# Holding back the fetches of the turned rows until the second and the fourth product of the second layer are computed

## The chip, the cores and the metric

One core of a Trainium2 chip runs the whole kernel. The metric is device time in microseconds (us), the median of several executions of the same program. TensorE (PE), VectorE (DVE), ScalarE (ACT) and GpSimd (POOL) each work through their own list of instructions in order; SyncE (SP) issues nearly all transfers (DMA), also in order. Between the engines stand semaphores. A matmul takes its stationary operand in a weight load (PEld) and streams the other one; all matrices are float32.

## The reference

Attention with random features, then a Fourier mix with a two-layer network, on 8 batches of 576 rows and 512 columns:

```
q_p, k_p = phi(q * scale), phi(k * scale)      # exp(h - max h), h = x @ omega.T - |x|^2 / 2
x   = (q_p @ (k_p.T @ v)) / (q_p @ sum(k_p) + 1e-6)      # heads side by side: (8, 576, 512)
u   = x + real(fft(fft(x, axis=1), axis=2))
un  = (u - mean(u)) / sqrt(var(u) + 1e-6)      # by rows
out = u + max(un @ w_ch1, 0) @ w_ch2           # w_ch1: 512 x 2048, w_ch2: 2048 x 512
```

## The kernel before

**Two stages.** The first stage (to about 424 us) does attention, the Fourier mix, the conversion of the weights and the network for the first 512 rows. The second stage does the network for the other 4096 rows, in eight blocks `j` of 512 rows. The change touches the second stage alone.

**A block.** Each layer of the network is one step of Strassen's scheme in Winograd's form: seven products of half-size matrices in place of eight, with sums of operands before and after. The first layer of a block (`first_of`, matmuls at L1310) goes through eight column groups `fc`, seven small products each. The second layer (`product_of`, matmuls at L1490) has seven products `i`, in the order `ORDER = (1, 2, 4, 5, 6, 7, 3)`, and each of these is once more split into seven **parts** `n`, in the order `PARTS = (1, 2, 5, 6, 3, 7, 4)`. "Part 4.1" is part n = 1 of product i = 4. So a block has 49 parts; a part is four matmuls (eight instructions in the trace, two passes of float32) and takes 0.893 us. Parts of neighbouring products are interleaved, and the first parts of a block's second layer run among the last products of its first layer; the next block's first layer starts among the last parts.

**Weights of the second layer.** The 49 pieces of a block's weights (256 KB each) are laid out in DRAM (`w2l`) and loaded anew for each block by `loads_w2` (issues at L1393, tile `wl`), product by product; loads are numbered #0 to #48 here, so #14 is part 4.1, #15 is 4.2, #28 is 6.1, #29 is 6.2 and #35 is 7.1. There are 12 buffers: load #n waits on SP until the (n-11)th part of the block in the order of execution has read its buffer.

**Operands of the parts.** Parts 5, 6, 7 and 3 of a product use four sums s1, s2, s3 and again s1, made by DVE in `add_up` (L1457). The last of them overwrites s1 and so must wait until part 5 has read it:

```
(s1, a(1, 0), a(1, 1), ALU.add, 5),
(s2, s1, a(0, 0), ALU.subtract, 6),
(s3, a(0, 0), a(1, 0), ALU.subtract, 7),
(s1, a(0, 1), s2, ALU.subtract, 3),
...
after = ready(0, 1) + ((me, "p5 read"),) * (n == 3)
```

So part 3 of a product needs: end of part 5, then one DVE addition of 128x512, then its own start. The results of the parts leave PSUM by ACT (L1465, L1523) and by DVE additions `added` (L1470). Whole products are added up by `plus` (L1530): 128x512 additions on POOL or DVE, POOL's starting as soon as ACT has written the last quarter of the product (L1523) and DVE the others.

**The turned rows.** The first layer needs the normalised rows transposed. For blocks 1 to 7 `norm_of` loads 128 rows (L1015), normalises them, DVE transposes 32x32 squares and SP stores the result in a DRAM tensor `turned` (L980). Once two such stores are done, `fetched(j, h, dst)` brings one half of the block back, reordered: four transfers of 128 KB (issues at L988, tile `unT`) for h = 0 and four for h = 1. Then `block_norms` makes four sums of the halves on DVE (L1171, tile `tt`), which the first layer of block j uses. The halves and the sums live in four slabs that come free when the first layer of block j - 1 ends; so both fetches, and the sums, take place during the second layer of block j - 1.

**What sets the order.** The kernel writes the whole order itself. Each piece of work is a `Step` with an engine, a planned duration, a planned delay of its result (`late`), the events it comes `after`, and for DMAs a size. `Listing.run` picks the step that could begin first by its own clock and appends it to its engine's list. `port=True` marks additions that the plan never lets DVE and POOL do at the same moment. The plan's events and times order the instructions; they do not become waits on the chip. There, semaphores are set only where data or buffers require it.

In the order before, the fetches of block j stand in SP's list directly behind load #13 (h = 0) and load #14 (h = 1) of the second layer of block j - 1.

Of the kernel before, what the change touches and what calls it, by code (L numbers as in the profile page):

```python
# [35 lines left out]
PE, ACT, DVE, POOL, SP, NONE = "pe", "act", "dve", "pool", "sp", "none"  # L36
# [244 lines left out]
def kernel(  # L281
# [685 lines left out]
    turned = {}  # L967
# [13 lines left out]

    def fetched(j, h, dst):
        yield Step(
            SP, 1.7, 3.0, after=(("turned", j, 2 * h), ("turned", j, 2 * h + 1)),
            makes=("unT", j, h), kb=330,
        )
        for g in range(4):
            nc.sync.dma_start(  # L988
                dst[Q * g : Q * g + Q].rearrange("q (b k) d t -> q b (k d t)", k=2),
                turned[j, h][:, g].rearrange("(b q) k n -> q b (k n)", q=Q),  # L990
            )
# [159 lines left out]
    def block_norms(j, pool):  # L1151
        t0 = (NPLAIN * TP + TB * j) // 128
        yield Step(NONE, take=("slab",) * 4, after=events_of(range(t0, t0 + TB // 128)) + ("converted",))
        un = unTs[j] = [slabs.tile([128, HT // Q, NDC, Q], F32, name="unT2", tag="slab") for _ in range(2)]
        tt = [slabs.tile([128, 2, HT // Q, D2, Q], F32, name="tt", tag="slab") for _ in range(2)]
        tts[j] = tt[0][:, 0], tt[0][:, 1], tt[1][:, 0]
        for i in range(TB // 128):
            h, k = divmod(i, HT // 128)
            if pool is mlpp:
                dst = un[h][:, 4 * k : 4 * k + 4].rearrange("p g d q -> p d g q")  # L1160
                yield Fork(norm_of(j, t0 + i, i, pool, dst))
            elif not k:
                yield Fork(fetched(j, h, un[h]))
        parts = TB // 128 if pool is mlpp else 2
        yield Step(NONE, after=tuple(("unT", j, i) for i in range(parts)), bias=1.54)
        ops = sums_right(
            un[0][:, :, 0:D2], un[1][:, :, 0:D2], un[0][:, :, D2:NDC], un[1][:, :, D2:NDC], *tts[j]
        )
        for i, (o, l, r, op) in enumerate(ops):
            yield Step(DVE, 0.6, makes=("tt", j) if i == 3 else None, port=True, bias=-0.49)  # L1170
            nc.vector.tensor_tensor(out=o, in0=l, in1=r, op=op)  # L1171
# [460 lines left out]
```

## Time and profile before

| | |
|---|---|
| median of 3 runs | 1171.0 us (1168.07 to 1171.58) |
| the profiled execution | 1174.67 us, span 1172.2 us |
| TensorE busy | 1153.5 us, 98% of the span; granted clock 0.996 |
| DVE, ACT, POOL busy | 64%, 37%, 37% |
| second stage, first to last matmul | 423.9 to 1167.8 us |
| part matmuls (L1490) | 3136 instructions, 275 ns mean, one every 0.112 us |
| DMA moved | 220.34 MB, mean 188 GB/s |

The busy share of a matmul engine whose instructions overlap says little on what it lost. In this kernel the losses of TensorE are read from the length of equal stretches of work: the same 368 instructions of the second layer take 41.1 us in one block and more in others.

### The profile page before, as it was taken

What the parts mean: (1) busy time and instruction counts of PE and PEld (TensorE: products, weight loads), DVE (VectorE), ACT (ScalarE), POOL (GpSimd) and SP (SyncE); (2) the same over time, 40 slices, a digit from 0 to 9 for tenths busy, and PEclk for the clock granted to TensorE, in tenths of its full rate; (3) what the DMA queues carried; (4) which work ended last, traced back from release to release, by engine and by line L of the source; (5) the groups of instructions that cost most, each with busy time, mean ns of one, the idle gap of its engine ahead of it and who ended that gap; (6) DMA issues with size and microseconds to landing.
All of it is one profiled execution on the core that took longest, in us unless ns stands there. A gap on an engine that the chain in (4) does not pass through costs nothing.

```text
span 1172.2 us, 31328 instructions
## 1 busy us (share of the span) xinstructions
PE 1153.5 (98%) x12437; PEld 1032.9 (88%) x12437; DVE 754.7 (64%) x1573; ACT 436.8 (37%) x1485; POOL 430.4 (37%) x496
## 2 busy tenths in 40 slices
PE   8999999999999999999999999999999999999998
PEld 7888888779777868998998998898999899899898
DVE  5999999986676655744754664573573574474255
ACT  6998898866444212122112212212212212221211
POOL 2433444455472106225225324413513512522421
PEclk8999999999999999999999999999999999999999
DMA  7866765665662254873783593694495396388055
GB/s 218 224 188 186 240 181 178 203 210 163 207 196 101 77 162 139 263 264 85 222 278 112 172 308 99 152 317 141 112 319 190 82 290 231 83 258 263 35 166 203
DMA packets 167217, 220.34 MB, mean 188 GB/s; under 512 B 50080, under 2 KB 81056, under 8 KB 167072
## 3 DMA queue, kind: packets, MB, share of 16 engines
q1 hardware_dynamic: 166576, 218.09, 60.7%
q8 instruction: 98, 1.61, 0.6%
q14 instruction: 47, 0.39, 0.1%
q10 hardware_dynamic: 496, 0.26, 0.1%
HBM read 179.24 MB, written 43.25 MB: 190 GB/s over the span
## 4 chain that ended last, share of the span: by engine, by line
PE 88%; DMA 5%; DVE 4%; ACT 2%; SPq 1%; issue 1%; DVEq 0%
PE banks L1310 33%; PE banks L1490 27%; PE banks L1099 5%; PE banks L606 5%; PE banks L1122 4%; PE banks L512 4%; DMA wl<-w2l 3%; PE banks L640 2%; PE banks L687 2%; PE banks L849 2%; PE banks L799 1%; ACT e L566 1%; DVE nmx L549 1%; DMA kq<-in_k_dram 1%; PE banks L809 1%; PE banks L860 1%
## 5 line engine op out<-in xcount | busy, mean ns | idle before, releaser
L1490 PE MATMUL banks<-wl,sums 128*128 128x128 f32 x1792 | 217.4, 275 | 0.0
L1490 PEld LDWEIGHTS banks<-wl,sums 128*128 128x128 f32 x1792 | 208.6, 192 | 0.0
L1296 DVE CUSTOM_DVE_ANT_0 hid<-banks,s 128x256 f32<-128x256 f32 x192 | 80.9, 424 | 188.8 <-PE banks L1310 188.8
L566 ACT ACTIVATE e<-banks,nmx 128x128 f32<-128x128 f32 x576 | 165.3, 434 | 23.2 <-DVE nmx L549 22.4
L1324 ACT ACTIVATE s<-banks 128x256 f32<-128x256 f32 x192 | 73.7, 384 | 259.0 <-PE banks L1310 259.0
L1310 PE MATMUL banks<-unT,w 128*128 128x256 f32 x704 | 166.3, 379 | 0.0
L1310 PEld LDWEIGHTS banks<-unT,w 128*128 128x128 f32 x704 | 133.2, 190 | 18.3 <-issue 0.5
L1530 POOL TENSOR_TENSOR ur<-ur,part 128x512 f32<-128x512 f32 x32 | 47.3, 1479 | 267.1 <-ACT part L1523 187.0
L1465 ACT ACTIVATE s<-banks 128x128 f32<-128x128 f32 x168 | 46.6, 278 | 256.7 <-PE banks L1490 220.3
L1310 PE MATMUL banks<-tt,w1s 128*128 128x256 f32 x512 | 126.3, 379 | 0.0
L1310 PEld LDWEIGHTS banks<-tt,w1s 128*128 128x128 f32 x512 | 97.0, 190 | 13.7 <-DVE hid L1296 0.4
L1490 PE MATMUL banks<-wl,hid 128*128 128x128 f32 x768 | 100.0, 276 | 3.2 <-DMA wl<-w2l 3.1
L1470 DVE TENSOR_TENSOR part<-banks,s 128x128 f32<-128x128 f32 x168 | 49.0, 292 | 83.4 <-PE banks L1490 82.2
L549 DVE TENSOR_REDUCE nmx<-banks 128x8 f32<-128x1024 f32 (+1 forms) x96 | 89.3, 951 | 19.7 <-PE banks L606 15.5
L1490 PEld LDWEIGHTS banks<-wl,hid 128*128 128x128 f32 x768 | 94.0, 192 | 6.0 <-DMA wl<-w2l 4.5
L606 PE MATMUL banks<-om,kqT 64*64 64x128 f32 (+1 forms) x2088 | 80.6, 278 | 1.9 <-ACT kv L656 1.2
L1310 PE MATMUL banks<-unT,w1s 128*128 128x256 f32 x320 | 79.5, 379 | 0.0
L606 PEld LDWEIGHTS banks<-om,kqT 64*64 64x64 f32 (+1 forms) x2088 | 65.8, 140 | 13.3 <-issue 4.3
L1490 PE MATMUL banks<-wl,hs 128*128 128x128 f32 x576 | 75.1, 275 | 0.5 <-DVE part L1470 0.4
L1490 PEld LDWEIGHTS banks<-wl,hs 128*128 128x128 f32 x576 | 70.1, 192 | 1.2 <-DVE part L1470 0.6
L1377 POOL TENSOR_TENSOR hs<-hid,hs 128x256 f32<-128x256 f32 x64 | 50.1, 784 | 57.2 <-issue 37.1
L1310 PEld LDWEIGHTS banks<-unT,w1s 128*128 128x128 f32 x320 | 60.4, 190 | 8.7
(128 smaller groups left out, 1914.6 us busy)
## 6 DMA issues: line engine op xcount, KB each, us to landing
wl<-w2l SPq DMA_DIRECT2D x392, 256.0 KB
raw<-in_moe_w_ch_dram SPq DMA_DIRECT2D x32, 512.0 KB
kq<-in_k_dram SPq DMA_DIRECT2D x32, 288.0 KB
kq<-in_q_dram SPq DMA_DIRECT2D x32, 288.0 KB
vd<-in_v_dram SPq DMA_DIRECT2D x32, 288.0 KB
u<-us SPq DMA_DIRECT2D x36, 256.0 KB
ur<-us SPq DMA_DIRECT2D x36, 256.0 KB
out_dram<-ur SPq DMA_DIRECT2D x34, 256.0 KB
```

Source lines behind the costliest of these rows:

```text
L512: nc.tensor.transpose(ps[:, (j - j0) * 128 : (j - j0 + 1) * 128], src(j), ident[:])
L549: nc.vector.tensor_reduce(nmx[:, :, 0:num], pps[:, :, 0 : MF * num].rearrange("p b (c m) -> p b c m", m=MF), axis=AX.X, op=ALU.max, negate ...
L566: nc.scalar.activation(out=e[:, c + (i if num == 1 else 0), :], in_=pps[:, i, MF * c : MF * c + MF], func=AF.Exp, bias=nmx[:, i, c : c + 1],)
L606: nc.tensor.matmul(pps[cols, c, MF * m : MF * m + MF], lhsT=kqT[rows, j, cols], rhs=om2[rows, :],)
L1099: nc.tensor.matmul(hp[:, 0:TP], lhsT=w1[:, dc, 128 * fc : 128 * fc + 128], rhs=unTs[key][:, dc, :], start=(dc == 0), stop=(dc == NDC - 1),)
L1296: nc.vector._custom_dve(TENSOR_ADD_SAT, out=o, in0=ps, in1=sb, s0=FMAX, s1=0.0)
L1310: nc.tensor.matmul(ps[:, 0:HT].rearrange("f (b q) -> f b q", q=Q), lhsT=left(dc), rhs=right(dc), start=start and dc == 0, stop=(dc == D2 - 1),
L1324: nc.scalar.activation(out=s[:], in_=ps[:, 0:HT], func=AF.Copy)
L1377: nc.gpsimd.tensor_tensor(out=o, in0=l, in1=r, op=op)
L1470: nc.vector.tensor_tensor(out=part[:, t, 128 * m : 128 * m + 128], in0=ps[:, 0:128], in1=saved[with_][:], op=ALU.add,)
L1490: nc.tensor.matmul(ps[:, 0:128], lhsT=left[:, f], rhs=wls[j, i, n][:, f], start=start and f == 0, stop=(f == 3), skip_group_check=True,)
L1530: eng.tensor_tensor(out=o, in0=o, in1=other, op=ALU.add)
```

## The change

The planned step of a fetch gets one more event to come after: the reading of product 2 of the running second layer for h = 0, of product 4 for h = 1 (`"read"` is made by the last part of a product; by `ORDER` these are the second and the third product to be computed). Its planned time on SP goes from 1.7 to 1.9 and its planned delay from 3.0 to 5.0.

```diff
     def fetched(j, h, dst):
         yield Step(
-            SP, 1.7, 3.0, after=(("turned", j, 2 * h), ("turned", j, 2 * h + 1)),
+            SP, 1.9, 5.0,
+            after=(("turned", j, 2 * h), ("turned", j, 2 * h + 1), (("second", j - 1, (2, 4)[h]), "read")),
             makes=("unT", j, h), kb=330,
         )
```

No operation is added or taken away. What changes is the order that the planner writes out for the second stage, in blocks 0 to 6 alike. On SP the fetch of h = 0 moves from behind load #13 to behind load #28, the fetch of h = 1 from behind #14 to behind #33. On DVE the four sums of L1171 move with them. The interleaving of the parts on TensorE changes, and of the eleven additions L1530 of a block POOL gets two where it had four, DVE nine where it had seven. Block 7, which fetches nothing, keeps its order on TensorE.

## The prediction

> **What bounds the kernel now.** I read the page's first part: TensorE is the engine that never rests.
>
> ```profile
> PE 1153.5 (98%) x12437; PEld 1032.9 (88%) x12437; DVE 754.7 (64%) x1573; ACT 436.8 (37%) x1485; POOL 430.4 (37%) x496
> ```
>
> The chain of waits gives TensorE 88% of the span and, in the second stage, almost nothing else but DMA of `wl`. So the question is what TensorE loses there. The table of stretches answers it: the same 368 instructions of L1490 (46 parts in a row) in blocks 1 to 6, 7 and 0. Columns: stretch, its length, PE busy, PEld busy, clock, DMA share, GB/s.
>
> ```profile
> 567.09:608.81 41.72, 41.52 (x368) 41.05 (x367) 1.00 0.97 304
> 659.84:701.15 41.31, 41.31 (x368) 40.97 (x367) 1.00 0.96 306
> 752.18:794.55 42.37, 41.36 (x368) 40.98 (x367) 1.00 0.96 300
> 845.58:887.27 41.69, 41.46 (x368) 41.04 (x367) 1.00 0.96 303
> 938.30:981.11 42.81, 41.42 (x368) 41.04 (x367) 1.00 0.94 295
> 1032.14:1074.15 42.01, 41.62 (x368) 41.05 (x367) 1.00 0.96 302
> 1125.18:1166.28 41.10, 41.09 (x368) 40.90 (x367) 1.00 0.73 237
> 474.35:516.06 41.71, 41.56 (x368) 41.05 (x367) 1.00 0.96 303
> ```
>
> Block 7 fetches nothing and takes 41.10; the other seven sum to 293.62, that is 293.62 - 7 x 41.10 = **5.92 us** lost. The loss is no larger elsewhere: outside these stretches the matmuls of the stage follow at their usual distance. SP's and TensorE's timelines of block 1 show where it falls:
>
> ```profile
> 566.62 1.85 SPq L988 DMA_DIRECT2D unT<-turned  x4
> 568.57 0.38 SPq L1393 DMA_DIRECT2D wl<-w2l  x1
> 569.05 1.80 SPq L988 DMA_DIRECT2D unT<-turned  x4
> 570.94 38.22 SPq L1393 DMA_DIRECT2D wl<-w2l  x45
> ...
> 576.39 2.05 PE L1490 MATMUL banks<-wl,hid 128*128 128x128 f32 x16 [0.20 <-DMA wl<-w2l]
> ```
>
> Both fetches (1 MB) stand in front of load #15, which is issued at 570.94; part 4.2 needs it as the 13th part of the block and waits until 576.39.
>
> **Part one: the wait that goes, -5.92.** In the new order loads #14 and #15 are issued with no fetch before them. The new order of parts equals block 7's up to part 7.6 (the 39th), so block 7 is the measured case: 4.1 comes 3.38 after the issue of #14 there (1126.10 to 1129.48) and doesn't wait. I take all 5.92, and keep a lower bound: five stretches lose 0.59 on average, two lose 1.27 and 1.71, above that 0.68 and 1.12 by hitches (in block 5 one issue at L988 took 1.41 in place of 0.42). Without them the gain would be 7 x 0.59 = 4.1.
>
> **Part two: the fetches at their new place.** Cost by a queue worked out on block 7's clock. A load of 256 KB at the saturated rate below is 0.68 us; the row of 588 to 600 is the stream undisturbed. (Columns: stretch, PE, PEld, DVE, ACT, POOL busy, clock, DMA share, GB/s.)
>
> ```profile
> 576.00:578.00 2.00, 1.80 (x16) 1.62 (x15) 0.60 (x3) 0.00 (x0) 0.00 (x0) 1.00 1.05 385
> 588.00:600.00 12.00, 12.00 (x110) 12.00 (x109) 8.57 (x16) 2.03 (x8) 3.32 (x2) 1.00 0.89 290
> ```
>
> Quarters of a fetch: its 1 KB packets run in block 1 from 568.04 to 574.79, with 1.26 us of loads among them, so (6.75 - 1.26) / 8 = 0.69 each; over the blocks 0.66 to 0.76; I take 0.70. Packets were served in the order of issue. A lone load has its last packet 2.38 after issue, and a waiting part starts 0.93 after that (575.46 to 576.39). New place: #28 issued at 1138.61 is in at 1140.99; fetch h = 0 runs to 1143.79, #29 to 1144.47, usable 1145.40; part 6.2 comes at 1146.45: slack 1.05. Loads #30 to #33 run to 1147.19, fetch h = 1 to 1149.99, #34 and #35 to 1151.35, usable 1152.28; part 7.1 comes at 1152.71: **slack 0.43**. So no regular wait; of the two hitches (0.25 + 0.69) about +0.9 is left. Bounds: 0, and the case of slower quarters below.
>
> The Trainium skill, "DMA: Bandwidth & Descriptors", section "Bandwidth", gives one core some 358 GB/s of HBM. The row above shows 385 for 2 us. By the page a load would take 0.73 and the seven loads #29 to #35 0.36 more: slack 0.07 in place of 0.43, still no wait, so the sum would stay.
>
> SP's list itself: behind a fetch stand only loads; the 1.85 us of issues are in the table above. The sums L1171 wait on DVE for h = 1: usable at 1149.99 + 0.93 = 1150.92, DVE reaches them at 1153.2; cover 2.3 us. The next first layer starts after part 3.6, some 7 us after the last sum. The two additions that go from POOL to DVE cost DVE 2 x 0.68 per block; DVE stood idle before its PSUM additions (0.5 to 1.2 us each in block 1's timeline), and nothing waits for L1530 soon.
>
> **Part three: a new wait at part 7.3.** Block 7 runs 7.5, 7.6, 3.1, 7.3; the new order of blocks 0 to 6 runs 7.5, 7.6, 7.3. So the last sum of product 7 (L1457) has one part's time, 0.893, and not two. Undisturbed: DVE starts 0.21 after 7.5 ends, adds 0.69, TensorE follows 0.045 later (as in the tail, 1166.61 to 1166.65): 0.945, so 0.05 late, plus 0.10 that TensorE's second instruction loses after each wait: 0.15. But POOL is in the way. Rows of block 1:
>
> ```profile
> 587.70 0.69 DVE L1457 TENSOR_TENSOR sums<-hs,sums 128x512 f32<-128x512 f32 x1
> 588.30 1.76 DVE L1457 TENSOR_TENSOR sums<-hs 128x512 f32<-128x512 f32 x1
> ...
> 587.82 1.69 POOL L1530 TENSOR_TENSOR ur<-ur,part 128x512 f32<-128x512 f32 x1 [18.33 <-ACT part L1523]
> ```
>
> POOL waits for DVE's running addition (588.39), ends 1.12 after it (589.51), and DVE's next one, 0.69 long elsewhere, ends 0.55 after POOL (590.06). In the new order POOL's addition of product 6 waits only for ACT's copy of 6.4's result: 6.4 ends 1156.28, ACT's next copy is 1156.48 to 1156.76, POOL starts 1156.83. DVE then holds the fourth sum L1171 (the third starts after 7.2's addition at 1155.86, the fourth 0.61 later: 1156.47 to 1157.15). POOL ends 1158.27, the sum of product 7, ready to start at 1157.38, ends 1158.82, part 7.3 starts 1158.87 in place of 1158.07. Wait 0.80 + 0.10 = 0.90; seven blocks: **+6.3**. The plan put these additions apart, but that is no wait on the chip. Bounds: 0.15 (1.05 in all; POOL out of the way) and 1.33 (9.3; POOL first, below).
>
> The Trainium skill, "SBUF — State Buffer", section "Who interferes with whom", says that an addition with two SBUF inputs and a GpSimd one exclude each other and the second blocks fully. By that the sum would run its whole 0.69 after POOL's end, 0.14 more than the row's 0.55: 7 x 1.04 = 7.3 in place of 6.3, and the sum 1 us higher.
>
> **Sum.** -5.92 + 6.3 + 0.9 = +1.3. The profiled execution would go from 1174.67 to 1176.0; it was 3.7 above the median, so on the median's scale 1171.0 + 1.3 = **1172.3**.
>
> **Rivals.** About 0.3% (3.5 us) can be told from no change: faster is below 1167.5, slower above 1174.5.
> - A, the forecast: one wait in place of another. Own range: 1171.0 - 5.92 + 5.1 (0.73 a block, if POOL runs 1.27 straight from 1156.83) = 1170.2, to 1171.0 - 4.1 + 6.3 + 0.9 = 1174.1. Chance 0.47.
> - B, faster: POOL and the sum miss each other, 7.3 waits 0.15. For it: POOL's spans are rough, and in block 7 POOL's addition fell at 1159.22, clear of the sums. Against it: there it waited for a DVE addition that has moved. 1171.0 - 5.92 + 1.05 + 0.9 = 1167.0. Chance 0.20.
> - C, slower: POOL gets in before the fourth sum L1171. It decides once that sum starts 0.36 later (1156.47 against 1156.83), as with a late fetch or a late third sum. POOL 1156.83 to 1158.10, fourth sum to 1158.65, product 7's sum to 1159.26, part 7.3 at 1159.30: 1.23 + 0.10, 9.3 in all. 1171.0 - 5.92 + 9.3 + 0.9 = 1175.3. Chance 0.22.
> - D, slower: in the full stream a quarter takes 0.85. Then #35 is 1.20 later, part 7.1 waits 0.77 + 0.10, in all 6.1: 1172.3 + 6.1 = 1178.4. For it: slack 0.43 only; against: 0.76 was the worst block. Chance 0.09.
> - E: the planner's event does nothing. The written order contradicts it. 1171.0, chance 0.02.
>
> **Numbers.** Predicted is A, 1172.3. The range 1166.0 to 1176.5 takes in B, A and C; what is left out is D and tails, some 0.15. Same: A without its edges, part of B and C, and E, 0.48; faster 0.18; slower 0.34 (most of C, D, A's upper edge).
>
> **What would show it.** In the profile after: the waits of TensorE for `wl` under 1 us in all, loads #14 and #15 without a fetch before them (right for part one); a wait of 0.7 to 0.9 on DVE L1457 at the 40th part of blocks 0 to 6, with a POOL L1530 that ends 0.55 before that sum does (part three); none at part 7.1 (part two). A wait of 0.05 there is B, of 1.2 C, a wait for `wl` at the 34th part D. The prediction is wrong if an engine not named here stops TensorE.

## The result, and the profile after

The changed kernel takes **1183.95 us** (median of 6 runs, 1178.94 to 1187.21) against 1169.78 (6 runs, 1168.07 to 1171.75) for the kernel before, measured side by side: ratio 1.0118, 95% interval 1.0092 to 1.0144. It is 14.2 us slower, and outside the range that was given. The profiled execution took 1183.3 us, its span is 1181.5 at a granted clock of 0.998; the span is 9.3 longer than that of the kernel before.

The new line of the code shifts the line numbers behind it by one: the part matmuls are L1491 now, the loads of `wl` L1394, the fetches L989, the operand sums L1458, the additions of products L1531. The first part of the page says as little as it did before:

```profile
PE 1154.1 (98%) x12437; PEld 1032.6 (87%) x12437; DVE 754.1 (64%) x1587; ACT 438.0 (37%) x1485; POOL 408.0 (35%) x482
```

TensorE's list of waits of the changed kernel names two things that cost the part matmuls more than half a microsecond (line, what was waited for: us in total, times, longest):

```profile
PE banks L1491 <- DMA wl<-w2l: 5.8, 7, 1.8
PE banks L1491 <- ACT s L1466: 5.3, 8, 0.7
```

A wait for `wl` is still there, and a second wait comes once in each of blocks 0 to 6 (the eighth in that line is part 6.2 of block 6, which waits for its load #29: last landing mark at 1061.32, start at 1061.45). The order of parts is block 7's up to the 39th part, so blocks can be compared by equal stretches. The stretches of the changed kernel below run from the 3rd part to the start of the 39th, in blocks 0 to 7 (columns: stretch, its length, PE busy, PEld busy, clock, DMA share, GB/s):

```profile
474.34:506.88 32.54, 32.20 (x288) 32.01 (x288) 1.00 0.95 294
568.00:600.90 32.90, 32.20 (x288) 32.01 (x288) 1.00 0.96 289
662.23:694.48 32.25, 32.21 (x288) 32.02 (x288) 1.00 0.96 290
755.59:787.97 32.38, 32.21 (x288) 32.02 (x288) 1.00 0.97 286
849.08:883.05 33.97, 32.20 (x288) 32.01 (x288) 1.00 0.94 281
944.16:978.27 34.11, 32.50 (x288) 32.15 (x288) 1.00 0.94 281
1039.60:1073.67 34.07, 32.44 (x288) 32.08 (x288) 1.00 0.95 282
1134.78:1166.72 31.94, 31.94 (x288) 31.94 (x288) 1.00 0.89 286
```

Block 7, which fetches nothing, takes 31.94. The other seven sum to 232.22, that is 232.22 - 7 x 31.94 = **8.64 us** lost to late weights (the list above shows less, since it counts idle time alone, not the 0.10 that TensorE's second instruction loses after each wait, and puts the one at 6.2 in block 6 down to ACT). From the start of the 39th part to that of the 41st the same blocks take 2.71 where block 7 takes 1.79: 0.93 a block, **6.5 us**.

Where the first loss falls is seen in block 5. SP's timeline of the changed kernel (start, length, what was issued, how many):

```profile
943.33 14.58 SPq L1394 DMA_DIRECT2D wl<-w2l  x16
957.96 1.85 SPq L989 DMA_DIRECT2D unT<-turned  x4
959.91 4.45 SPq L1394 DMA_DIRECT2D wl<-w2l  x5
964.59 1.83 SPq L989 DMA_DIRECT2D unT<-turned  x4
966.80 18.33 SPq L1394 DMA_DIRECT2D wl<-w2l  x22
```

TensorE's timeline there (in brackets the idle time and what ended it):

```profile
973.76 1.16 PE L1491 MATMUL banks<-wl,hid 128*128 128x128 f32 x8 [1.04 <-DMA wl<-w2l]
...
980.08 2.02 PE L1491 MATMUL banks<-wl,sums 128*128 128x128 f32 x16 [0.69 <-ACT s L1466]
```

Loads #14 and #15 stand in the row of 16 with no fetch in front of them. The row at 973.76 is part 7.1 (load #35, behind the fetch of h = 1), the row at 980.08 part 7.3. That second wait is put down to ACT, which had long been done. DVE's timeline shows what it was:

```profile
977.62 0.68 DVE L1172 TENSOR_TENSOR tt<-unT,tt 128x512 f32<-128x512 f32 x1
978.53 1.44 DVE L1458 TENSOR_TENSOR sums<-hid,sums 128x512 f32<-128x512 f32 x1 [0.23 <-PE banks L1491]
```

And POOL's:

```profile
978.00 1.44 POOL L1531 TENSOR_TENSOR part<-part 128x512 f32<-128x512 f32 x1 [4.51 <-ACT part L1524]
```

POOL starts 0.38 after DVE's fourth sum of the turned rows and ends at 979.44. The sum that part 7.3 needs takes 1.44 in place of 0.69, ends at 979.97, 0.53 after POOL, and part 7.3 starts 0.11 later.

### The profile page after: what moved, and what is told of

It reads as the page before. It is cut to its first block, busy times and chain, and to the rows that moved or that the text cites. A ratio compares the mean times of both kernels' runs of the same rounds, so it can differ in the third digit from the quotient of the medians.

```text
span 1181.5 us, 31259 instructions
## 1 busy us (share of the span) xinstructions
PE 1154.1 (98%) x12437; PEld 1032.6 (87%) x12437; DVE 754.1 (64%) x1587; ACT 438.0 (37%) x1485; POOL 408.0 (35%) x482
## 4 chain that ended last, share of the span: by engine, by line
PE 84%; DMA 7%; DVE 4%; ACT 2%; SPq 1%; issue 1%; POOL 0%; DVEq 0%
PE banks L1311 33%; PE banks L1491 26%; DMA wl<-w2l 5%; PE banks L1100 5%; PE banks L1123 4%; PE banks L512 4%; PE banks L606 4%; PE banks L640 2%; PE banks L687 2%; PE banks L849 2%; PE banks L799 1%; DVE nmx L549 1%; DMA raw<-in_moe_w_ch_dram 1%; ACT e L566 1%; DMA kq<-in_k_dram 1%
## 5 line engine op out<-in xcount | busy, mean ns | idle before, releaser
L1491 PE MATMUL banks<-wl,sums 128*128 128x128 f32 x1792 | 220.2, 275 | 4.8 <-ACT s L1466 4.8
L1491 PEld LDWEIGHTS banks<-wl,sums 128*128 128x128 f32 x1792 | 210.2, 192 | 6.3 <-ACT s L1466 6.0
L1297 DVE CUSTOM_DVE_ANT_0 hid<-banks,s 128x256 f32<-128x256 f32 x192 | 77.3, 418 | 153.6 <-PE banks L1311 153.6
L1311 PE MATMUL banks<-tt,w1s 128*128 128x256 f32 x512 | 123.4, 379 | 0.0
L1491 PE MATMUL banks<-wl,hid 128*128 128x128 f32 x768 | 100.8, 276 | 5.3 <-DMA wl<-w2l 5.2
L1491 PEld LDWEIGHTS banks<-wl,hid 128*128 128x128 f32 x768 | 94.6, 192 | 7.9 <-DMA wl<-w2l 6.6
L1378 POOL TENSOR_TENSOR hs<-hid 128x256 f32<-128x256 f32 x64 | 46.6, 729 | 138.5 <-DVE hid L1297 138.1
L1531 POOL TENSOR_TENSOR ur<-ur,part 128x512 f32<-128x512 f32 x11 | 13.9, 1265 | 208.4 <-ACT part L1524 199.8
L1491 PE MATMUL banks<-wl,hs 128*128 128x128 f32 x576 | 76.4, 276 | 1.4 <-DMA wl<-w2l 0.6
L1491 PEld LDWEIGHTS banks<-wl,hs 128*128 128x128 f32 x576 | 70.6, 192 | 2.2 <-ACT s L1466 1.3
L1378 POOL TENSOR_TENSOR hs<-hid,hs 128x256 f32<-128x256 f32 x64 | 50.2, 784 | 63.9 <-ACT hid L1363 41.7
```

What stands on the lines that cost most here:

```text
L1297: nc.vector._custom_dve(TENSOR_ADD_SAT, out=o, in0=ps, in1=sb, s0=FMAX, s1=0.0)
L1311: nc.tensor.matmul(ps[:, 0:HT].rearrange("f (b q) -> f b q", q=Q), lhsT=left(dc), rhs=right(dc), start=start and dc == 0, stop=(dc == D2 - 1),
L1378: nc.gpsimd.tensor_tensor(out=o, in0=l, in1=r, op=op)
L1491: nc.tensor.matmul(ps[:, 0:128], lhsT=left[:, f], rhs=wls[j, i, n][:, f], start=start and f == 0, stop=(f == 3), skip_group_check=True,)
```

## The experiments

In experiments 1, 2, 3, 4, 5, 6, 7 and 8 the order of the second stage is a written list, as the planner had made it for the changed kernel or the kernel before, and the edit changes an entry of the list or the transfers; line numbers differ there for that reason. All times are medians; ratios are against runs of the kernel before beside them (its median was 1168.9 to 1170.2 in all sets but that of experiment 12). The second stage of the profiled executions begins at 423.8 us in the kernel before and 424.0 in the changed one, but at 418.4 to 420.9 in the experiments, whose first stage is the same. So where single executions are compared below, it is by the length of the second stage, from its first matmul (L1310 in the kernel before) to the end of the span: 748.4 us in the kernel before, 757.6 in the changed one. What the profiles show adds up to that difference: -5.92 + 8.64 + 6.5 = 9.2. The medians lie 14.2 apart.

**Experiment 1: the addition that holds up part 7.3 goes to DVE.**

```diff
 # the changed kernel's order, blocks 0 to 6: product 6 added to product 1's sum
-POOL plus
+DVE  plus   (behind product 5's)
```

> The changed kernel's written order, with one addition of blocks 0 to 6 (product 6 into the sum of product 1, L1530 of before) done by DVE behind the addition of product 5 instead of by POOL; nothing else moves. Theory (the sum of product 7 waits for POOL's addition, 0.92 us a block): the wait at part 7.3 falls from 0.92 to about 0.15, 7 x 0.77 = 5.4 us less, 1183.95 to about 1178.5. Rival (part 7.3 waits because its sum stands too late on DVE, whatever POOL does): the wait stays near 0.9 and the time near 1184.

Measured: 1179.01 (1173.37 to 1181.88), ratio 1.0075 (1.0053 to 1.0097). The timelines of this kernel in block 5, TensorE's:

```profile
965.95 1.16 PE L1668 MATMUL banks<-wl,hid 128*128 128x128 f32 x8 [1.54 <-DMA wl<-w2l]
...
969.63 3.91 PE L1668 MATMUL banks<-wl,sums 128*128 128x128 f32 x32
```

and DVE's:

```profile
970.72 0.69 DVE L1635 TENSOR_TENSOR sums<-hid,sums 128x512 f32<-128x512 f32 x1 [0.23 <-PE banks L1668]
```

The sum takes 0.69 again, and 7.5, 7.6, 7.3 run on in one row of 32 instructions. Part 7.3 comes 0.10 late, its second instruction 0.07 more: 0.17 a block are left of 0.93. The wait for `wl` in front of 7.1 stays. So the clash of POOL and DVE is worth 1183.95 - 1179.01 = 4.9, though the runs of either kernel scatter by 8 us; experiment 6 repeats the step with less scatter.

**Experiment 2: part 3.1 in front of 7.3.**

```diff
 # the changed kernel's order of parts, blocks 0 to 6
-7.5, 7.6, 7.3, 7.7, 3.1, 7.4
+7.5, 7.6, 3.1, 7.3, 7.7, 7.4
```

> The changed kernel's written order, with part 3.1 moved in front of part 7.3 on TensorE in blocks 0 to 6 (7.6, 3.1, 7.3, 7.7), as in block 7; POOL's addition stays. Theory: the sum of product 7 is as late as before, but one part of 0.89 us covers the wait of 0.92: it falls to nearly 0, 7 x 0.9 = 6.3 us less, about 1177.5. Rival (the loss is in the loads and only shows at 7.3): it turns up at the next parts, the time stays near 1184.

Measured: 1182.25 (1181.47 to 1183.58), ratio 1.0103 (1.0087 to 1.0119): 1.7 less than the changed kernel, within the scatter, where 6.3 were expected. The wait at 7.3 is gone, but TensorE's timeline of this kernel has another one two parts later:

```profile
503.23 1.99 PE L1668 MATMUL banks<-wl,sums 128*128 128x128 f32 x16
505.60 1.16 PE L1668 MATMUL banks<-wl,hid 128*128 128x128 f32 x8 [0.38 <-DVE part L1648]
```

Parts 7.3 and 7.7 run through; 7.4 then waits for an addition on DVE that reads PSUM (L1648), which could itself begin only when 7.7 was done. It comes in each of blocks 0 to 6 and costs 0.55 + 0.10. The code says why: part 4 of a product adds on to the PSUM bank that part 7 wrote, and comes `after` the addition `c22`, which reads that bank in between. In the changed kernel's blocks 0 to 6 something always stands between a product's parts 7 and 4, and between 7.7 and 7.4 it was 3.1. Where nothing does, at 3.7 and 3.4 at the end of block 7, the same wait of 0.55 + 0.10 is in the changed kernel too:

```profile
1176.26 1.16 PE L1491 MATMUL banks<-wl,hs 128*128 128x128 f32 x8 [0.38 <-DVE part L1471]
```

The miss teaches that a part may not be moved by its own operands alone. The waits for `wl` are also larger in this kernel's profile, 11.4 us in the list where the changed kernel has 5.8; why was not tried.

**Experiments 3 and 4: a half fetched in one transfer.** In both kernels the rows of a half come in another order, so what is computed from block 1 on is not the reference; bytes and all other work are the same.

```diff
-        for g in range(4):
-            nc.sync.dma_start(
-                dst[Q * g : Q * g + Q].rearrange("q (b k) d t -> q b (k d t)", k=2),
-                turned[j, h][:, g].rearrange("(b q) k n -> q b (k n)", q=Q),
-            )
+        nc.sync.dma_start(
+            dst[:].rearrange("p b d t -> p (b d t)"),
+            turned[j, h][:].rearrange("p g k n -> p (g k n)"),
+        )
```

In the changed kernel's order:

> The changed kernel's written order, with each half fetched by one transfer of 128 rows of 4 KB in place of four of 1 KB pieces: same bytes, same place, rows in another order, so what is computed from block 1 on is not the reference's. Theory (the loads behind a fetch are late because four issues and 1 KB pieces hold the queue some 2.8 us per half, in a stream that has little room): 512 KB at 385 GB/s is 1.36 us, the waits for wl at parts 6.2 and 7.1 (8.6 us in the profiled execution) fall under 1.5, time about 1176.5; the wait of 0.92 at part 7.3 stays. Rival (the bytes and the place decide, not the form): waits of 6 us or more, time about 1183.

In the order before:

> The kernel before, with the same one transfer per half (computes another order of rows from block 1 on). It asks what the fetches cost the kernel before when it is not profiled. If as in its profiled execution: 5.9 us less, about 1164. If the profiled execution, 4.9 above the median, overstates them: 1 us less, about 1168.8. In both the profile's waits for wl fall under 1 us in all.

Measured: 1171.88 (1170.82 to 1175.15), ratio 1.0019 (1.0007 to 1.0031), and 1165.47 (1163.77 to 1167.06), ratio 0.9959 (0.9943 to 0.9975). No wait for `wl` is left in blocks 0 to 6 of either (one of 0.3 is in block 7 of experiment 3, which fetches nothing). So the form of the fetch costs 1183.95 - 1171.88 = 12.1 in the changed kernel and 1169.9 - 1165.5 = 4.4 in the kernel before, by medians. The second stages of the profiled executions give 757.6 - 749.9 = 7.7 and 748.4 - 742.6 = 5.8. By both it costs more at the new place than at the old one; how much more is known to some 3 us only.

**Experiment 5: four transfers of whole rows.** One transfer differs from four in the number of issues, in the size of the pieces and in how many partitions each fills. Here the pieces are 4 KB, the rest is as in the changed kernel (rows in another order, as in experiment 3).

```diff
+        for g in range(4):
+            nc.sync.dma_start(
+                dst[Q * g : Q * g + Q].rearrange("p b d t -> p (b d t)"),
+                turned[j, h][Q * g : Q * g + Q].rearrange("p g k n -> p (g k n)"),
+            )
```

> The changed kernel's order; each half is still fetched by four transfers, but each brings 32 whole rows of 4 KB (in another order, so what is computed from block 1 on is not the reference) in place of 1 KB pieces. The one transfer of 4 KB rows took 12.1 us off the changed kernel (1183.95 to 1171.9). If it was the size of the pieces that made part 7.1 late, nearly all of that comes again: 1172 to 1174, no wait for wl above 0.2 us. If it was the number of issues that SP has to get through (8 in place of 2 per block), the waits at 7.1 stay: about 1180 to 1184. In between, both count.

Measured: 1182.12 (1176.86 to 1184.62), ratio 1.0100 (1.008 to 1.012). The size of the pieces is not it.

**Experiment 6: both edits, of experiments 1 and 3.**

> The changed kernel's order with both edits: a half in one transfer of 4 KB rows (so not the reference from block 1 on), and product 6's addition on DVE in place of POOL. If the two losses are separate and are all that the change costs, the sum closes: 1171.9 less the wait at part 7.3, of 6.5 in the profile and 5.0 by the medians of the earlier runs: 1165.4 to 1166.9, as the kernel before has with the fetch in one (1165.5). If the order has a third cost, it stays above 1168.

Measured: 1166.85 (1164.95 to 1167.62), ratio 0.9973 (0.9963 to 0.9983). The account closes: 1183.95 - 12.1 - 4.9 = 1166.95, and what is left above experiment 4 (1.4) is about the 7 x 0.17 = 1.2 that part 7.3 loses undisturbed. From experiment 3 to this one the clash is worth 1171.88 - 1166.85 = 5.0. No third cost shows above the scatter.

**Experiment 7: the fetch of h = 0 at its old place, h = 1 held back.**

```diff
 # SP's list of the changed kernel, blocks 0 to 6
-#13, #14, ... #28, fetch h = 0, #29, ... #33, fetch h = 1
+#13, fetch h = 0, #14, ... #33, fetch h = 1
```

> The changed kernel's order, but the fetch of h = 0 stands on SP where it stood before (behind load #13, four transfers of 1 KB pieces); only h = 1 is held back, behind #33. If the two fetches have to share one lead of the loads (some 5.6 us of extra transfer between #28 and #35), half of it is absorbed: no wait at 7.1, none at 4.2 either, and the clash at 7.3 stays: 1171.5 to 1174. If a fetch of 1 KB pieces right in front of #34 and #35 is enough by itself, the waits at 7.1 stay at half a microsecond or more per block: 1176 to 1184.

Measured: 1182.53 (1179.18 to 1184.49), ratio 1.0109 (1.0091 to 1.0127). Neither theory had this. SP's timeline of this kernel in block 5:

```profile
941.88 0.32 SPq L1570 DMA_DIRECT2D wl<-w2l  x1
942.26 2.70 SPq L1165 DMA_DIRECT2D unT<-turned  x4
945.06 11.61 SPq L1570 DMA_DIRECT2D wl<-w2l  x13
```

and TensorE's:

```profile
948.90 1.16 PE L1667 MATMUL banks<-wl,hid 128*128 128x128 f32 x8 [1.72 <-DMA wl<-w2l]
```

The waits at 7.1 are gone in all blocks: one fetch in front of #34 is absorbed. But the changed order runs part 4.1 as its 8th part, two earlier than the order before, and 4.1 needs load #14, which now stands behind the fetch: 1.1 to 1.9 are lost there in every block, 10.1 idle in all. So at 7.1 it takes both fetches together, and the old place of h = 0 only fits the old order of parts.

**Experiments 9 and 10: four transfers, each to all partitions.** (The numbers are those of the runs' names; 8 follows at the end.) Issues, bytes, 1 KB pieces and what is computed stay; a transfer takes one block of 32 rows of DRAM and spreads it over all partitions.

```diff
-        for g in range(4):
+        for b in range(4):
             nc.sync.dma_start(
-                dst[Q * g : Q * g + Q].rearrange("q (b k) d t -> q b (k d t)", k=2),
-                turned[j, h][:, g].rearrange("(b q) k n -> q b (k n)", q=Q),
+                dst[:, 2 * b : 2 * b + 2].rearrange("p k d t -> p (k d t)"),
+                turned[j, h][Q * b : Q * b + Q].rearrange("q g k n -> g q (k n)"),
             )
```

In the changed kernel:

> The changed kernel with the fetch's four transfers cut another way: each brings 1 KB to every one of the 128 partitions in place of 4 KB to 32 of them. The number of issues (four per half), the bytes and the 1 KB pieces stay, and so does what is computed. If the wait for wl at part 7.1 comes from transfers that fill only 32 partitions (in the profile of the run with four transfers of 4 KB rows a 4 KB packet took 0.27 to 0.29 us where it took 0.18 with all partitions), it goes: 1171.5 to 1174, with the wait of 0.9 at 7.3 left. If it is four issues in place of one, it stays: 1180 to 1184.

In the kernel before:

> The kernel before with the same edit of the fetch, nothing else: if the 32 partitions are the cause, its waits at part 4.2 go as with the fetch in one transfer: 1164 to 1166.5. If the issues are, SP still gets to load #15 only 4.3 us after load #13: 1168.5 to 1170.5.

Measured: 1247.79 (1240.52 to 1252.05), ratio 1.0674 (1.0644 to 1.0704), and 1238.76 (1236.85 to 1239.61), ratio 1.0597 (1.0578 to 1.0617). Stretches of experiment 10 in which the fetch ran (PE, PEld, DVE, ACT, POOL busy, clock, DMA share, GB/s):

```profile
472.50:474.50 2.00, 2.00 (x20) 2.00 (x19) 1.99 (x5) 0.32 (x2) 0.69 (x1) 1.00 0.22 76
476.00:478.00 2.00, 1.04 (x10) 0.85 (x8) 1.61 (x5) 0.28 (x1) 0.00 (x0) 1.00 0.27 89
479.00:481.00 2.00, 0.68 (x5) 0.68 (x6) 0.00 (x0) 0.00 (x0) 0.00 (x0) 0.99 0.27 90
```

A quarter of the DMA engines is busy: the packet records show 4 packets of the fetch running at a time, of 0.05 us each, where the old form keeps 13 going in the kernel before and 11 in the changed one (medians). The source's outermost dimension is 4 here (`g`), and 4 engines do the work. The Trainium skill, "DMA: Bandwidth & Descriptors", section "Why a DMA increments its semaphore by 16 and not by 1", says just this: the number of engines is the largest, up to 16, that divides the slowest dimension of both sides. So these two runs don't answer their question.

**Experiment 11: the same with the source spread too.** Each transfer reads one 1 KB piece of each of 128 rows (another order, as in experiment 3).

```diff
+                dst[:, 2 * g : 2 * g + 2].rearrange("p k d t -> p (k d t)"),
+                turned[j, h][:, g].rearrange("p k n -> p (k n)"),
```

> The changed kernel; a half in four transfers of 128 KB, each 1 KB to every partition, read from one row each of 128 rows of DRAM (in another order, so not the reference from block 1 on). Issues, bytes and the 1 KB pieces are those of the changed kernel; what differs is that each transfer fills 128 partitions, not 32, and is spread over all engines of the queue, which the run with pieces taken four rows apart was not (there 4 packets ran at a time). If 32 partitions are the cause of the waits at 7.1: 1171.5 to 1174, no wait for wl. If it is four issues in place of one: 1180 to 1184. If it is the 1 KB pieces together with the issues, in between.

Measured: 1171.83 (1170.39 to 1175.92), ratio 1.0021 (1.0008 to 1.0035): experiment 3's time with four issues and 1 KB pieces. Two of the stretches from the 3rd to the 39th part, blocks 4 and 5 of this kernel:

```profile
843.69:875.63 31.94, 31.94 (x288) 31.94 (x288) 1.00 0.91 290
936.74:968.67 31.93, 31.93 (x288) 31.93 (x288) 1.00 0.92 295
```

They are as long as block 7's; they were 33.97 and 34.11. What the queue moves while the fetch of h = 1 passes, in the changed kernel:

```profile
966.30:968.30 2.00, 2.00 (x18) 2.00 (x19) 0.29 (x1) 0.00 (x0) 0.00 (x0) 1.00 0.97 242
968.30:970.30 2.00, 2.00 (x20) 2.00 (x19) 1.73 (x5) 0.28 (x1) 0.00 (x0) 1.00 1.10 218
970.30:972.30 2.00, 2.00 (x20) 2.00 (x20) 1.27 (x3) 0.56 (x2) 0.08 (x1) 1.00 1.04 318
```

and in experiment 11, from the same distance behind the issue:

```profile
957.70:959.70 2.00, 2.00 (x21) 2.00 (x20) 0.73 (x2) 0.28 (x1) 0.00 (x0) 1.00 0.89 292
959.70:961.70 2.00, 2.00 (x21) 2.00 (x19) 1.51 (x3) 0.28 (x1) 0.00 (x0) 1.00 1.05 347
961.70:963.70 2.00, 2.00 (x20) 2.00 (x19) 1.49 (x3) 0.40 (x2) 0.00 (x0) 1.00 1.05 388
```

The DMA share is about 1 in both: in the changed kernel the engines are as busy and move 218 GB/s where they move 347. The number of issues and the size of the pieces are the same (experiments 3 and 5 say the same of whole rows), so what slows a packet is that it goes to 32 neighbouring partitions; whether their number or their place counts is the next question.

**Experiment 12: which partitions.** Rows in another order, as in experiment 3.

```diff
+        for g in range(4 if h else 2):
+            rows = slice(g, P, 4) if h else slice(64 * g, 64 * g + 64)
+            n = 32 if h else 64
+            nc.sync.dma_start(
+                dst[rows].rearrange("p b d t -> p (b d t)"),
+                turned[j, h][n * g : n * g + n].rearrange("p g k n -> p (g k n)"),
+            )
```

> The changed kernel; the rows of a half come in another order (not the reference from block 1 on), whole rows of 4 KB. h = 0 comes in two transfers to 64 neighbouring partitions each, h = 1 in four transfers to 32 partitions each that lie four apart (0, 4, ... 124). So far a 4 KB packet took 0.28 us in transfers to 32 neighbouring partitions and 0.18 in one transfer to all 128. If what counts is how many partitions a transfer fills, h = 0 comes out between the two and h = 1 at 0.28, with the waits at 7.1 as they were: 1178 to 1184. If it is that neighbouring partitions lie behind few of the memory's ports, h = 0 stays at 0.28, as 64 neighbours reach no more than 32 do, and h = 1 gets shorter, down to 0.18 if its 16 engines write to different ports at each moment: then the waits at 7.1 shrink, 1172 to 1178.

Measured: 1171.77 (1169.6 to 1174.14) beside 1166.12 for the kernel before, ratio 1.0045 (1.003 to 1.006); this set's runs of the kernel before lie 3 to 4 us under those of the other sets. The profile is plainer: TensorE's list of waits no longer names `wl` at all, the seven waits at 7.3 are there, and the second stage takes 749.2 us, as in experiments 3 and 11 (749.9 and 749.4). By the ratios some 3 us are left above those two, which the second stage doesn't show. The median length of a fetch packet, by the packet records:

| transfer to | packet | us | run |
|---|---|---|---|
| 32 neighbouring partitions | 1 KB | 0.075 | changed kernel |
| 128 partitions | 1 KB | 0.046 | 11 |
| 32 neighbouring partitions | 4 KB | 0.280 | 5 |
| 64 neighbouring partitions | 4 KB | 0.242 | 12, h = 0 |
| 32 partitions four apart | 4 KB | 0.161 | 12, h = 1 |
| 128 partitions | 4 KB | 0.159 | 3 |

For h = 1 it is not the number of partitions but which: 32 that lie four apart are as good as 128. The Trainium skill, "SBUF — State Buffer", section "Door 1: The DMA port swizzle (why `[64,N]` ≈ `[32,N]`)", has the rule: bits of the partition number choose one of 16 ports, partitions 0 to 31 reach 8 of them and 0 to 63 no more; it measured 189 GB/s for 32, in a transfer of 1 MiB. The prediction's quarter, 128 KB in 0.70 us, is 187 GB/s. The runs agree with the page on 32 neighbours and on 32 that lie four apart. For 64 neighbours they don't settle it: 0.242 is shorter than 0.280, and by blocks the median runs from 0.160 to 0.280.

**Experiment 8: the order before, with the turned rows laid out to be fetched in one transfer.** What is computed is the reference. Each store of 128 rows goes out as four of 32 partitions, with the same 512-byte pieces, at a time when SP has little to do.

```diff
-            turned[j, h] = dram.tile([P, 4, 2, NDC * Q], F32, name=f"turned{j}_{h}")
+            turned[j, h] = dram.tile([4, Q, 4, 2, NDC * Q], F32, name=f"turned{j}_{h}")
...
-        nc.sync.dma_start(t[:, :, k], w[:].rearrange("p g d q -> p g (d q)"))
+        for b in range(4):
+            nc.sync.dma_start(
+                t[:, :, b, k].rearrange("g q n -> q g n"),
+                w[Q * b : Q * b + Q].rearrange("p g d q -> p g (d q)"),
+            )
...
+        nc.sync.dma_start(
+            dst[:].rearrange("p b d t -> p (b d t)"),
+            turned[j, h][:].rearrange("g q b k n -> (g q) (b k n)"),
+        )
```

> The order of the kernel before, the reference in full: the turned rows lie in DRAM so that a half is fetched in one transfer of 4 KB rows; for that each store of 128 rows goes out as four transfers of 32 partitions with the same 512-byte pieces. If the fetch's form is what costs, and three more issues per store hide in SP's idle time of the first layer, the time is that of the run with rows in another order: 1165 to 1167. If the stores' issues delay the first loads of wl or the rows, 1168 to 1173.

Measured: **1163.9** (1163.27 to 1166.32) beside 1170.15, ratio 0.9957 (0.9943 to 0.997). It beats both kernels; its second stage takes 742.3 us, where experiment 4 has 742.6. SP's timeline of this kernel in block 5:

```profile
925.13 2.87 SPq L1158 DMA_DIRECT2D turned<-turn  x4
929.14 0.34 SPq L1573 DMA_DIRECT2D wl<-w2l  x1
929.54 0.42 SPq L1168 DMA_DIRECT2D unT<-turned  x1
930.90 0.32 SPq L1573 DMA_DIRECT2D wl<-w2l  x1
931.39 0.32 SPq L1168 DMA_DIRECT2D unT<-turned  x1
```

Each fetch is one issue, the loads follow at once, and nothing in the second stage waits for `wl`.

## Why the prediction was wrong, step by step

**Part one, the wait that goes: mechanism right, size not excluded.** Loads #14 and #15 have no fetch before them and parts 4.1 and 4.2 don't wait. The 5.92 was the loss of one profiled execution. By the medians of experiment 4 the fetches cost the kernel before 4.4, and the interval of its ratio, 2.9 to 6.7 us, holds both 5.92 and the lower bound of 4.1.

**Part two, the fetches at their new place: this step failed.** "Slack 0.43. So no regular wait" is wrong: part 7.1 waits in every block, in blocks 5 and 6 part 6.2 too, and 8.64 us are lost in the profile (12.1 by medians) against 0.9. The term that was mis-sized is the first of the sum: "#28 issued at 1138.61 is in at 1140.99". It gives a load in the full stream the 2.38 of a lone one. The traces hold sixteen landing marks for each transfer, and in the changed kernel part 7.1 starts 0.04 to 0.05 after the last mark of load #35 in each block, so the last mark tells when a load can be used. The sum reckons 2.38 + 0.93 = 3.31 for that. But in block 7 of the kernel before, whose clock the sum uses, #28 has its last mark at 1143.07, 4.46 after its issue. With this and the other terms as they stood, part 7.1 would have waited some 0.8. In blocks 0 to 6 the terms came out so (us, each from last mark to last mark, mean, in brackets lowest and highest):

| term | reckoned | changed kernel | experiment 11 |
|---|---|---|---|
| #28, from its issue | 3.31 | 4.67 (3.88 to 5.92) | 3.79 (3.42 to 4.21) |
| fetch h = 0 | 2.80 | 2.31 (2.10 to 2.47) | 1.90 (1.44 to 2.55) |
| #29 to #33 | 3.40 | 4.44 (3.67 to 5.09) | 4.52 (4.13 to 5.06) |
| fetch h = 1 | 2.80 | 2.41 (2.16 to 3.02) | 1.56 (1.44 to 1.94) |
| #34 and #35 | 1.36 | 1.36 (1.11 to 2.15) | 1.56 (1.33 to 2.21) |
| in all | 13.67 | 15.19 (14.26 to 16.13) | 13.34 (12.84 to 13.87) |

Part 7.1 is due 14.10 after the issue of #28. So on average the halves were not slower than reckoned; the loads in front of each half were late. Beyond #28 the errors nearly cancel: +1.04 for the five loads against -0.49 and -0.39 for the halves. "Packets were served in the order of issue" does not hold for a transfer as a whole: the sixteen marks of #28 lie 1.3 to 3.5 apart, those of #33 1.1 to 3.9, and in block 5 the half behind #33 has its first mark at 967.49, #33 its last at 970.33. Experiment 11 has the same order and the same number of issues, fills all partitions, and stays under 14.10 in every block: its #28 lands late too, but the rest makes up for it. Why #28 lands later in front of a slow fetch than in front of a fast one stays open.

**Rival D came nearest, in part by luck.** It put the wait at 7.1 in the full stream and priced it 0.87 a block, 1178.4 in all, with a chance of 0.09, since "0.76 was the worst block". The loss is 8.64 / 7 = 1.23 a block. The place was right, but its cause, quarters of 0.85, is not what the marks show: 2.31 and 2.41 for four of them. What had to be doubted was the delay of a load taken from a place where it ran alone.

**Part three, the new wait at 7.3: right.** 0.90 a block and 6.3 in all were forecast; 0.93 and 6.5 are in the profile. The chain holds row by row: the fourth sum in front, POOL 0.38 after its start (0.36 forecast), the sum 0.53 after POOL's end (0.55), the part behind it. Undisturbed, 0.17 is left (0.15). By medians the clash is 4.9 with the other loss and 5.0 without it.

**The sum.** By medians -4.4 + 12.1 + 5.0 + 1.2 = +13.9, measured +14.2. By the two profiles -5.92 + 8.64 + 6.5 = +9.2, and the spans differ by 9.3. The forecast had -5.92 + 0.9 + 6.3: by either account the 0.9 is what was wrong.

## What to carry to other kernels

The rate of a transfer belongs to what it fills and what runs beside it: before a transfer is moved into a full queue, see which partitions it writes, and look for late loads in front of it as well as behind. A slack of half a microsecond that rests on a delay taken from a lone load is no slack: read the landing of that very load in the full stream. Compare stages, not whole executions, where only one stage was changed. Where a wait depends on a slow transfer, change its shape first; its place can then often stay.

## What the runs showed of the hardware that was not expected

- Halves fetched in four transfers of 128 KB to 32 neighbouring partitions cost the changed kernel 12 us by medians (7.7 in the profiled second stage) against halves fetched in one transfer to all partitions. Four transfers that each fill all partitions cost no more than the one (1171.83 and 1171.88). A 4 KB packet to 32 partitions four apart took 0.161 us, to 128 partitions 0.159, to 32 neighbours 0.280.
- In block 7 of the kernel before, with no fetch near, load #28 took 4.46 us from its issue to its last landing mark; the sixteen marks of one load lay up to 3.9 us apart in the changed kernel (#33 of block 6).
- In experiment 10 transfers whose outermost source dimension is 4 kept 4 packets going, at a DMA share of 0.22 to 0.27: 76 to 90 GB/s, and 70 us more for the kernel before (1238.76 against 1168.94).
- Behind the long stalls of experiments 9 and 10 the granted clock fell to 0.50. Experiment 9, the stretches around its first long stall of block 0:

```profile
491.00:493.00 2.00, 0.23 (x3) 0.04 (x1) 0.19 (x1) 0.28 (x1) 0.00 (x0) 1.00 1.08 260
493.00:495.00 2.00, 0.31 (x1) 0.34 (x2) 0.00 (x0) 0.00 (x0) 0.00 (x0) 0.74 0.41 134
495.00:497.00 2.00, 2.00 (x11) 2.00 (x11) 0.15 (x1) 0.00 (x0) 0.00 (x0) 0.50 0.29 102
```

After some 3.5 us without matmuls it is 0.50, and 11 matmuls pass in 2 us in place of 20. So the kernel loses more than its waits: 50.2 us of idle time for `wl`, but 76.0 us against experiment 11. The waits of up to 1.8 us in the changed kernel left the clock at 1.00.
